# Attention turns of a retention and bilinear feed-forward kernel, rewritten as one burst of 64x64 matmuls over four quadrants of the array

## The chip, the core and the metric

The kernel runs on one core of a Trainium2 chip. A core has a matrix engine (TensorE, in the profile PE, with its weight loads as PEld), a vector engine (VectorE, DVE), a scalar engine (ScalarE, ACT), a general engine (GpSimd, POOL), a queue engine that issues transfers (SyncE, SP) and 16 DMA engines. Matmuls write into PSUM, which has eight banks of 128 partitions by 512 float32 numbers; the other engines read the banks and write into SBUF.

The metric is the time of one execution on the device in microseconds. Three executions of the kernel before gave 220.25, 220.42 and 220.65 us, a median of 220.42.

## The reference

```python
q, k, v: (4, 8, 768, 64)                       # batch, heads, sequence, head width
gamma = 1.0 - 2.0 ** (-5.0 - arange(8))
for t in range(768):                           # per batch and head
    state = gamma * state + outer(k[t], v[t])
    y[t] = (1 / 8) * q[t] @ state
x = y.transpose(0, 2, 1, 3).reshape(3072, 512)
out = ((x @ w_a) * (x @ w_b)) @ w_out          # (512, 1536), (512, 1536), (1536, 512)
```

The first half is a linear attention with a decay for each head, the second a feed-forward block without an activation function. All inputs and the output are float32; the kernel multiplies in bfloat16.

## The kernel before, in words

The sequence is cut into 24 slots of 128 tokens (4 batches of 6 slots). Instead of stepping through the tokens, the kernel folds the decay into two tables that scale keys and queries, and then works on a slot in four steps, all on PE, all with 64-wide heads:

- `scores`: keys times queries, 128 keys by 128 queries for each of 8 heads, as 16 products of 64 keys by 128 queries. They go to two PSUM banks, one for each parity `r` of the head. Then DVE multiplies each bank with a triangular mask into `aT`, so a product of a late key with an early query is computed and set to zero.
- `update`: keys times values, added to the running state `st` in PSUM (8 products, full 128 rows by 64 columns, 64 moving columns), after which an engine casts the state to `gst`.
- `inter`: the state of the slots before times the queries (8 products of 64x64, 128 moving columns), into the banks `y0` and `y1`.
- `intra`: values times the masked scores (8 products, 128 rows by 64 columns, 128 moving columns), into the same banks. `leave` then copies `y0` and `y1` with two ACT instructions to `xt`, the input of the feed-forward block.

Slots are taken in pairs. `turn(new, old)` does the scores and updates of the pair that begins with slot `new`, and the inter and intra products of the pair `old`, whose scores stem from an earlier turn. Eleven calls of `turn` carry slots 6 to 23 (pairs 3 to 11): T1 `turn(6, None)`, T2 `turn(None, 6)`, T3 `turn(8, None)`, T4 `turn(10, 8)`, T5 `turn(12, 10)`, T6 `turn(14, 12)`, T7 `turn(16, 14)`, T8 `turn(18, 16)`, T9 `turn(20, 18)`, T10 `turn(22, 20)` and T11 `turn(None, 22)`. Slots 0 to 5 go through functions of their own (`scores2`, `update2`, `inter2`, `intra2`), which this change touches in the name and the shape of one tile only.

Around the turns runs the feed-forward block over seven tiles of 4, 2, 2, 2, 2, 4 and 8 slots. `ffn_ab` is one step of it: four products into a bank for `a`, which ACT casts to `asb`, and four into a bank for `g`, which DVE multiplies with `asb` into `ht`. The tiles of two slots have 256 moving columns, those of four have 512. The output product of the middle tiles is done in seven products instead of eight (`Group`, with sums `hs` made on POOL or DVE); `single` laces one such group with the first steps of the next tile. Its arguments are the banks that it uses.

Three things set the order of the work. All instructions of an engine run in the order in which the program writes them (`seq`), so the order by hand at the end of the kernel is the order on each engine. PSUM is the second: three banks, `ff0` to `ff2`, form a ring (`Ring`) for the feed-forward products. `tile` takes the bank that has been idle longest in program order; `back` puts a bank at the end of the row as soon as the instruction that empties it has been written. The other five banks are `at0`, `at1`, `y0`, `y1` and `st`. A matmul into a bank waits on the chip until whoever emptied it is done. The third is that PE takes its matmuls in order, so a matmul that waits holds up all that follow.

Of the kernel before, what the change touches and what calls it, by code (L numbers as in the profile page):

```python
# [9 lines left out]
F32 = mybir.dt.float32  # L10
BF16 = mybir.dt.bfloat16
# [13 lines left out]
def kernel(  # L25
# [44 lines left out]
    class Ring:  # L70
# [143 lines left out]
    mask = const.tile([P, 1, P], BF16, name="mask")  # L214
    gst = [const.tile([P, HP, D], BF16, name=f"gst{i}") for i in range(4)]

    def late_tables():
        seq(nc.gpsimd.memset(mask, 1.0))
        seq(nc.gpsimd.affine_select(out=mask, in_=mask, compare_op=ALU.is_ge, fill=0.0, base=0,
                                    pattern=[[0, 1], [1, 2], [2, 64]], channel_multiplier=-1))  # L220
        tables([[P, NCH], [0, 1]], 1)
# [107 lines left out]
    def scores(t, where):  # L329
        at = score_banks(where)  # L330
        for hp in range(HP):
            for c in range(2):
                for r in range(2):
                    seq(nc.tensor.matmul(at[r][half(c), hp, :],  # L334
                                         kqT[t // 2][half(r), t % 2, 0, hp, half(c)],
                                         kqT[t // 2][half(r), :, 1, hp, half(t % 2)],
                                         start=True, stop=True, skip_group_check=True))
        aT[t] = tra.tile([P, 2, HP, P], BF16, tag="aT", name="aT")
        for r in range(2):
            seq(nc.vector.tensor_tensor(aT[t][:, r], at[r], mask.to_broadcast([P, HP, P]), op=ALU.mult))  # L340
        psff.back(*at)

    def update(t, eng):
        ci = t % NCH
        if ci == NCH - 1:
            return
        if ci == 0:
            state[0] = psst.tile([P, HP, D], F32, tag="st", name="st")
        st = state[0]
        for hp in range(HP):  # L350
            for r in range(2):
                seq(nc.tensor.matmul(st[half(r), hp, :], kb[t][:, hp, r, :],  # L352
                                     vb[t][:, HP * r + hp, :],
                                     start=(ci == 0 and hp == 0), stop=(hp == HP - 1),
                                     skip_group_check=True))
        cast(eng, gst[(t + 1) % 4], st)

    ys, begun = {}, set()

    def begin(t, *q):  # L360
        fresh = (t // 2, *q) not in begun
        begun.add((t // 2, *q))
        return fresh

    def inter(t):
        if t % NCH == 0:
            return
        for j in range(2):
            for c in range(2):
                for r in range(2):  # L370
                    hp = 2 * j + c
                    seq(nc.tensor.matmul(ys[t // 2][r][half(c), j, :, t % 2, :],
                                         gst[t % 4][half(r), hp, :],
                                         kqT[t // 2][half(r), :, 1, hp, half(t % 2)],
                                         start=begin(t, c, r), stop=False, skip_group_check=True))

    def intra(t):
        for r in range(2):
            for j in range(2):
                for c in range(2):  # L380
                    hp = 2 * j + c
                    seq(nc.tensor.matmul(ys[t // 2][r][half(c), j, :, t % 2, :],  # L382
                                         vb[t][:, HP * r + hp, :], aT[t][:, r, hp, :],
                                         start=begin(t, c, r), stop=True, skip_group_check=True))

    def leave(t):
# [5 lines left out]
        for r in range(2):  # L392
            seq(nc.scalar.copy(xt[key][:, 2 * r : 2 * r + 2, i * P : (i + 2) * P],  # L393
                               ys[t // 2][r].rearrange("p j a s n -> p j (a s n)")))

    def turn(new, old, eng=nc.scalar):
        if old is not None:
            ys[old // 2] = [psat.tile([P, 2, 2, 2, P // 2], F32, tag=f"y{r}", name="y") for r in range(2)]
        two = new is not None and (new + 1) % NCH < NCH - 1
        if new is not None:  # L400
            if two or old is None:
                update(new, eng)
            scores(new + 1, "y" if old is None else "ff")
            scores(new, "at")
        if old is not None:
            inter(old)
            inter(old + 1)
        if two:
            update(new + 1, nc.scalar)
        elif new is not None and old is not None:  # L410
            update(new, eng)
        if old is not None:
            intra(old)
            intra(old + 1)
            leave(old)


    kqT2 = {}
# [23 lines left out]
    def scores2(u, par, where="at"):  # L442
# [9 lines left out]
        aT[t] = tra.tile([P, 2, HP, P], BF16, tag="aT", name="aT")  # L452
        for r in range(2):
            seq(nc.vector.tensor_tensor(aT[t][:, r], at[r], masks[par].to_broadcast([P, HP, P]),
                                        op=ALU.mult))
# [29 lines left out]
    def intra2(u, par, begin):  # L485
# [3 lines left out]
        for hp in range(HP):  # L489
            for r in range(2):  # L490
                for c in range(2):
                    seq(nc.tensor.matmul(ys[u][c][half(r), hp, :], vb[t][half(c), 2 * hp + r, :],
                                         aT[t][half(c), r, hp, :],
                                         start=(begin and hp == 0), stop=not begin,
                                         skip_group_check=True))
# [25 lines left out]
    def ffn_a(J, ft, c0=0, c1=None):  # L521
# [11 lines left out]
        psff.back(bank)  # L533

# [89 lines left out]
    class Group:  # L624
# [141 lines left out]
    class Unit:  # L766
# [21 lines left out]
        def snap(self, n):  # L788
            pool, tag = ((tra, "aT"), (osbp, "osb"), (osbp, "osb"))[n]
            self.snaps[n] = pool.tile([P, 4 * P], F32, tag=tag, name=f"snap{n}")  # L790
# [64 lines left out]
    def big():  # L855
# [5 lines left out]
        def do(x):  # L861
            if x in plains:
                plain(*plains[x])
            elif x == "T":
                turn(None, 22)
# [131 lines left out]
    turn(6, None, V_)  # L997
# [5 lines left out]
    turn(None, 6)  # L1003
# [6 lines left out]
    turn(8, None)  # L1010
# [4 lines left out]
    turn(10, 8)  # L1015
# [35 lines left out]
    turn(16, 14)  # L1051
    blocks(4, 11, NFT)
    hsums(4, 3, 6, G_)
    casts(19)
    single(4, Y0, AT0, FF)
# [50 lines left out]
```

## Time and profile before

| what | value |
|---|---|
| time, median of three executions | 220.42 us |
| the profiled execution's own time | 220.34 us |
| its span on the core | 218.6 us |
| PE busy | 211.6 us (97%), 2242 matmuls |
| DVE, ACT, POOL busy | 138.9, 99.5 and 142.1 us |
| granted TensorE clock | full in all 40 slices |

The span runs from the first to the last instruction that the profile records; 1.7 us of the execution lie around it. In lists by line, the columns are the line of the kernel, engine, operation, tiles, shape and count, then the busy time and the mean duration of one in ns, then the idle time of the engine just before them. In a timeline each row is one run of like instructions: its start and its length in us, the engine, the line, and the count. A matmul's duration holds the time that it needs to pass through the array; the next one may start long before it ends, so the pace is read from starts, not from durations.

### The profile page before, as it was taken

How to read it: one execution, taken by the hardware profiler on the slowest of the kernel's cores; microseconds unless marked ns; L12 is line 12 of the kernel's file. 1: busy time of each engine (PE TensorE's matmuls, PEld its weight loads, DVE VectorE, ACT ScalarE, POOL GpSimd, SP SyncE). 2: the span in 40 equal slices, each digit the busy share in tenths (PEclk: the TensorE clock that was granted, in tenths of full speed). 3: DMA queues.
4: the chain of work that ended last, by engine and by line, in shares of the span. 5: the costliest groups of instructions: out<-in, count | busy, mean ns of one | idle time of the engine just before them, and what ended most of it. 6: DMA issues, size and time to landing. Idle time of an engine off the chain costs nothing.

```text
span 218.6 us, 5641 instructions
## 1 busy us (share of the span) xinstructions
PE 211.6 (97%) x2242; PEld 143.6 (66%) x2242; DVE 138.9 (64%) x253; ACT 99.5 (46%) x218; POOL 142.1 (65%) x163
## 2 busy tenths in 40 slices
PE   7789999999999999999999999999999999999994
PEld 3557445687458888888888655556865444448883
DVE  3776346845883485455377246976595777789642
ACT  3256335343234445464576245455535665632331
POOL 5265876779445587669765949999999985520000
PEclk9999999999999999999999999999999999999999
DMA  6999999999999999999999999940022000000055
GB/s 163 290 321 364 385 320 357 380 250 242 201 258 249 278 188 216 132 225 244 209 186 232 208 212 218 266 73 4 3 96 96 0 1 3 0 0 1 27 192 168
DMA packets 85146, 39.68 MB, mean 182 GB/s; under 512 B 57472, under 2 KB 78848, under 8 KB 85120
## 3 DMA queue, kind: packets, MB, share of 16 engines
q1 hardware_dynamic: 84976, 39.26, 79.9%
q8 instruction: 17, 0.28, 0.5%
q10 hardware_dynamic: 144, 0.07, 0.1%
q14 instruction: 9, 0.07, 0.1%
HBM read 28.31 MB, written 6.29 MB: 158 GB/s over the span
## 4 chain that ended last, share of the span: by engine, by line
PE 90%; SPq 4%; DMA 4%; POOL 0%; issue 0%; DVE 0%; ACT 0%
PE g L541 19%; PE a L529 19%; PE mA L645 12%; PE uA L785 8%; PE mB L645 6%; PE o L566 5%; PE uB L785 4%; DMA wstb<-in_moe_w_b_dram 4%; SPq L127 3%; PE mC L645 3%; PE at L334 2%; PE uC L785 2%; PE y L382 2%; PE st L352 2%; PE ka L844 2%; PE kb L844 2%
## 5 line engine op out<-in xcount | busy, mean ns | idle before, releaser
L543 DVE TENSOR_TENSOR ht<-g,asb 128x256 bf16<-128x256 f32 (+1 forms) x74 | 37.2, 503 | 37.1 <-PE g L541 34.2
L529 PE MATMUL a<-xt,wa_bf 128*128 128x256 bf16 (+1 forms) x296 | 52.7, 305 | 0.1
L541 PE MATMUL g<-xt,wb_bf 128*128 128x256 bf16 (+1 forms) x296 | 52.5, 304 | 0.2 <-POOL wb_bf L240 0.2
L532 ACT CAST asb<-a 128x256 bf16<-128x256 f32 (+1 forms) x74 | 32.3, 437 | 39.1 <-PE a L529 35.7
L541 PEld LDWEIGHTS <-wb_bf 128*128 128x128 bf16 x296 | 28.6, 98 | 12.8 <-POOL wb_bf L240 0.3
L529 PEld LDWEIGHTS <-wa_bf 128*128 128x128 bf16 x296 | 28.0, 98 | 12.2 <-POOL wa_bf L240 0.4
L281 POOL TENSOR_TENSOR kqb<-kf,ktab 128x512 bf16<-128x512 f32 x22 | 23.2, 1056 | 16.3 <-DMA kf<-in_k_dram 9.7
L645 PEld LDWEIGHTS <-hs 128*128 128x128 bf16 x240 | 23.4, 98 | 3.9
L340 DVE TENSOR_TENSOR aT<-at,mask 128x512 bf16<-128x512 f32 x36 | 22.3, 682 | 0.3
L791 ACT COPY snap<-uA 128x512 f32<-128x512 f32 x30 | 16.7, 587 | 12.6 <-PE uA L785 12.6
L281 POOL TENSOR_TENSOR kqb<-qf,qtab 128x512 bf16<-128x512 f32 x18 | 19.5, 1082 | 3.3 <-DMA qf<-in_q_dram 3.3
L652 ACT COPY snaps<-mA 128x256 f32<-128x256 f32 x30 | 11.2, 374 | 19.4 <-PE mA L645 19.3
L579 POOL TENSOR_TENSOR hs<-ht,hs 128x384 bf16<-128x384 bf16 (+1 forms) x17 | 16.7, 987 | 4.8 <-DVE ht L543 4.8
L645 PEld LDWEIGHTS <-ht 128*128 128x128 bf16 x180 | 17.5, 98 | 2.8
L579 POOL TENSOR_TENSOR ht<-gsb,asb 128x512 bf16<-128x512 bf16 x12 | 13.6, 1156 | 5.7 <-DVE gsb L579 5.7
L579 POOL TENSOR_TENSOR hs<-ht 128x384 bf16<-128x384 bf16 (+2 forms) x12 | 13.8, 1150 | 4.0 <-DVE ht L543 4.0
L645 PE MATMUL mA<-wsum,hs 128*128 128x256 bf16 x120 | 15.7, 273 | 0.0
L240 POOL CAST vb<-vf 128x512 bf16<-128x512 f32 x16 | 10.0, 642 | 7.4 <-DMA vf<-in_v_dram 7.2
L579 DVE TENSOR_TENSOR osb<-mB,snaps 128x256 f32<-128x256 f32 x20 | 8.4, 422 | 9.5 <-PE mB L645 5.1
L566 PE MATMUL o<-wo_bf,ht 128*128 128x512 bf16 x48 | 10.7, 379 | 0.0
L393 ACT CAST xt<-y 128x512 bf16<-128x512 f32 x18 | 9.7, 588 | 0.6 <-PE y L382 0.4
L579 DVE TENSOR_TENSOR gsb<-uB,snap 128x512 bf16<-128x512 f32 x10 | 6.9, 686 | 4.0 <-ACT snap L791 3.4
(104 smaller groups left out, 327.1 us busy)
## 6 DMA issues: line engine op xcount, KB each, us to landing
qf<-in_q_dram SPq DMA_DIRECT2D x12, 512.0 KB, 6.0
out_dram<-osb SPq DMA_DIRECT2D x21, 256.0 KB, 4.0
kf<-in_k_dram SPq DMA_DIRECT2D x18, 256.0 KB, 4.5
vf<-in_v_dram SPq DMA_DIRECT2D x18, 256.0 KB, 5.2
wsta<-in_moe_w_a_dram SPq DMA_DIRECT2D x6, 512.0 KB, 7.9
wstb<-in_moe_w_b_dram SPq DMA_DIRECT2D x6, 512.0 KB, 8.2
wsto<-in_moe_w_out_dram SPq DMA_DIRECT2D x6, 512.0 KB, 8.8
kf<-in_k_dram SPq DMA_DIRECT2D x3, 512.0 KB, 7.1
```

The lines of the kernel that those rows point to most:

```text
L281: seq(eng.tensor_tensor(dst, src, tab, op=ALU.mult))
L340: seq(nc.vector.tensor_tensor(aT[t][:, r], at[r], mask.to_broadcast([P, HP, P]), op=ALU.mult))
L529: seq(nc.tensor.matmul(a, wa_bf[:, kt, fs], xcols(J, kt, c0, c1), start=(kt == 0), stop=(kt == KT - 1)))
L532: seq(nc.scalar.copy(asb, a))
L541: seq(nc.tensor.matmul(g, wb_bf[:, kt, fs], xcols(J, kt, c0, c1), start=(kt == 0), stop=(kt == KT - 1)))
L543: seq(nc.vector.tensor_tensor(ht[J][:, ft, c0:c1], g, asbs.pop((J, ft, c0)), op=ALU.mult))
L566: seq(nc.tensor.matmul(o, ht[J][:, ft, i * P : (i + 1) * P], wo_bf[:, ft], start=(ft == 0), stop=(ft == NFT - 1), skip_group_check=True))
L579: seq(eng.tensor_tensor(dst, x, y, op=op))
L645: seq(nc.tensor.matmul(m, w, right[:, j], start=(first and j == 0), stop=(j == NP - 1), skip_group_check=True))
L652: seq(nc.scalar.copy(self.snaps[:, n], self.bank["A"]))
L785: seq(nc.tensor.matmul(m, w, right[:, k], start=(first and k == 0), stop=(k == 1), skip_group_check=True))
L791: seq(nc.scalar.copy(self.snaps[n], self.bank["A"]))
```

## The change

A turn becomes one `Burst`. Each of its products is 64 rows by 64 columns, so that four fit in the array at once: two halves of rows (keys, or heads for products that contract over the head width) by two halves of columns. The program keeps a list for each of the four quadrants (a lane), and `issue` writes the products in the order in which four clocks, one for each lane, reach them (56 for a product of 128 moving columns, 32 for one of 64).

- The scores: a product has 64 queries instead of 128. For each head and slot there are two products on the diagonal (`at`) and one of early keys with late queries (`off`, in two more banks); late keys with early queries are left out. That makes 48 products of 64 columns for a pair in place of 32 of 128. ACT copies each `off` bank to `aT`; DVE multiplies each `at` bank, which now holds both slots, with a mask `tri` of 64 columns: two DVE instructions for a pair in place of four.
- The intra products contract over 64 keys instead of 128: 40 products for a pair (8 of 128 columns and 32 of 64) in place of 16 of 128 columns with 128 rows. Part of the early values is copied to the other half of the partitions by two DVE copies for a pair (`early`).
- The first update of a turn joins the burst as 16 products of 64 rows; a second one follows the burst as before, and the cast of the state after it is put off to the next `ffn_a` or `turn` (`later`, `catch_up`).
- Products of the two row halves must not write a bank at the same time. A `token` is a product of 4 columns into a bank taken from the ring; from the second token on, the bank is taken anew (`renew`), so that the token waits for the one before. Between two row halves in a bank lie at least two tokens.
- Where a turn has both a new and an old pair (T4 to T10), the two `off` banks come from the ring, as does the bank of the tokens, which is taken first. In T1 and T3 `off` uses `y0` and `y1`.
- `leave` copies `y0` with ACT and `y1` with DVE, but with ACT alone in T2 and T11. Slots 7 and 9 are updated one turn later. T7 moves behind the last step and the sums of its tile, directly before `single(4, ...)`, whose banks `AT0` and `Y0` change places.
- In the last group of the kernel the two halves of the last row go to two tiles `osb` in place of one; two tiles take other buffers (`aT2`, `snap`).

```diff
+        def renew(self, old, shape, dtype, name):
+            n = next(n for n, (x, _) in enumerate(self.out) if x is old)
+            tag = self.out[n][1]
+            self.out[n] = ffpool.tile(shape, dtype, tag=tag, name=name), tag
+            return self.out[n][0]
...
-    mask = const.tile([P, 1, P], BF16, name="mask")
+    tri = const.tile([P, 1, 64], BF16, name="tri")
...
+    class Burst:
+        def __init__(self):
+            self.lists = {(row, c): [] for row in range(2) for c in range(2)}
+            self.left, self.then = {}, {}
+            self.spot = psff.tile([P, 4], F32, tag="ff", name="token")
...
+        def token(self, row, c):
+            def make():
+                if self.tokens:
+                    self.spot = psff.renew(self.spot, [P, 4], F32, "token")
+                return nc.tensor.matmul(self.spot[half(c)], ident[half(row), half(c)], ident[half(row), :4],
+                                        start=True, stop=True, skip_group_check=True)
...
+        def issue(self):
+            clock = {x: 0 for x in self.lists}
+            self.tokens, user = 0, {}
+            while any(self.lists.values()):
+                lane = min((x for x in self.lists if self.lists[x]), key=lambda x: (clock[x], x))
+                bank, cols, make, what = self.lists[lane].pop(0)
+                clock[lane] += 56 if cols > 64 else 32
+                if bank is None:
+                    continue
+                seq(make())
...
+                row, since = user.get(bank, (lane[0], 0))
+                assert row == lane[0] or self.tokens >= since + 2, (bank, what)
...
+            psff.back(self.spot)
...
+        def scores(self, u, row, at, off, hps=range(4)):
...
+            for hp in hps:
+                for s in range(2):
+                    for c in range(2):
+                        self.add(row, c, f"at{row}", 64,
+                                 product(at[row][half(c), hp, s], s, hp, c, c), ("S", row))
+                    self.add(row, hp // 2, f"off{row}", 64,
+                             product(off[row][half(hp // 2), hp % 2, s], s, hp, 0, 1), ("S", row))
...
+        later.append(lambda: cast(nc.scalar, gst[(t + 1) % 4], state[0]))
...
-        for r in range(2):
-            seq(nc.scalar.copy(xt[key][:, 2 * r : 2 * r + 2, i * P : (i + 2) * P],
-                               ys[t // 2][r].rearrange("p j a s n -> p j (a s n)")))
-
-    def turn(new, old, eng=nc.scalar):
+        for r, eng in enumerate(on):
+            cast(eng, xt[key][:, 2 * r : 2 * r + 2, i * P : (i + 2) * P],
+                 ys[t // 2][r].rearrange("p j a s n -> p j (a s n)"))
+
+    def turn(new, old, updates=None, eng=nc.scalar, on=(nc.scalar, nc.vector)):
+        catch_up()
+        x = Burst()
...
+        if new is not None:
+            u = new // 2
+            offs = score_banks("ff" if old is not None else "y")
...
+            def left(r):
+                seq(nc.scalar.copy(aT[u][:, r, HP:], off[r]))
+                seq(nc.vector.tensor_tensor(aT[u][:, r, :HP].rearrange("p h s n -> p (h s) n"),
+                                            at[r].rearrange("p h s n -> p (h s) n"),
+                                            tri.to_broadcast([P, 2 * HP, 64]), op=ALU.mult))
+                if old is not None:
+                    psff.back(offs[r])
...
+        for row in range(2):
+            if new is None:
+                x.inter(old, row)
+                x.inter(old + 1, row)
+                x.intra(o, row, row)
+                x.token(row, row)
+                x.rest(row, 1 - row)
+                x.intra(o, row, 1 - row)
+                continue
+            if row == 0:
+                if first is not None:
+                    x.update(first, 0, "u0")
+                    x.token(0, 0)
+                if old is not None:
+                    x.intra(o, 0, 1)
+                    x.token(0, 1)
+                x.scores(u, 0, at, off)
+            else:
+                if old is not None:
+                    x.intra(o, 1, 0)
+                x.scores(u, 1, at, off, range(1))
+                if old is None:
+                    x.scores(u, 1, at, off, range(1, HP))
+                if first is not None:
+                    x.token(1, 1)
+                    if old is None:
+                        x.rest(1, 0)
+                    x.update(first, 1, "u0")
+                if old is not None:
+                    x.scores(u, 1, at, off, range(1, HP))
+                    x.token(1, 0)
+            if old is not None:
+                x.inter(old, row)
+                x.inter(old + 1, row)
+                x.intra(o, row, row)
+        x.issue()
+        if second is not None:
+            update(second)
+        if new is not None:
+            for s in range(2):
+                src = vb[new + s][:64].rearrange("p (r hp) d -> p r hp d", r=2)[:, :, 2:]
+                seq(nc.vector.tensor_copy(early[u][64:, s], src))
+        if old is not None:
+            leave(old, on)
...
-                    c = slice(DH + n * P, DH + (n + 1) * P)
-                    cast(eng, self.row(0)[:, c], self.bank["A"][:, n * P : (n + 1) * P])
-                    seq(queue.dma_start(out=last_row[:, c], in_=self.osb[0][:, c]))
+                    c = slice(n * P, (n + 1) * P)
+                    osb = osbp.tile([P, P], F32, tag="osb", name="osb")
+                    cast(eng, osb, self.bank["A"][:, c])
+                    seq(queue.dma_start(out=last_row[:, DH + n * P : DH + (n + 1) * P], in_=osb))
...
-    turn(16, 14)
     blocks(4, 11, NFT)
     hsums(4, 3, 6, G_)
+    turn(16, 14)
     casts(19)
-    single(4, Y0, AT0, FF)
+    single(4, AT0, Y0, FF)
```

More of the change, by code (lines that the diff above doesn't have):

```diff
@@ L350, in update @@
+    def update(t):
         for hp in range(HP):
             for r in range(2):
[L352 to L354 removed]
+                seq(nc.tensor.matmul(state[0][half(r), hp, :], kb[t][:, hp, r, :],
+                                     vb[t][:, HP * r + hp, :], start=False, stop=(hp == HP - 1),
                                      skip_group_check=True))
[L356 removed]
@@ L358 @@
[L358 to L375, printed above, removed]
@@ L387, in leave @@
+    def leave(t, on):
         J, i = where[t]
@@ L400, in turn @@
+        x.issue()
+        if second is not None:
+            update(second)
         if new is not None:
[L401 to L404, printed above, removed]
+            for s in range(2):
+                src = vb[new + s][:64].rearrange("p (r hp) d -> p r hp d", r=2)[:, :, 2:]
+                seq(nc.vector.tensor_copy(early[u][64:, s], src))
         if old is not None:
-            inter(old)
@@ L407, in turn @@
[L407 to L418, printed above, removed]
+            leave(old, on)
+    kqT2, aT2 = {}, {}
     def casts2(u, on, between=None):
```

142 lines of the change are left out of this document (100 added, 42 removed).

## The prediction

> **What bounds the kernel now.** I read the page first (span, busy shares, granted clock), then the busy time by stretch, then the timeline of PE over single turns. The first fence is from the page, the second from the table of stretches.
>
> ```profile
> span 218.6 us, 5641 instructions
> ...
> PE 211.6 (97%) x2242; PEld 143.6 (66%) x2242; DVE 138.9 (64%) x253; ACT 99.5 (46%) x218; POOL 142.1 (65%) x163
> ...
> PEclk9999999999999999999999999999999999999999
> ```
>
> ```profile
> 66.00:121.00 55.00, 55.00 (x773) 47.88 (x772) 31.07 (x65) 28.36 (x72) 38.29 (x40) 1.00 1.25 216
> 121.00:149.00 28.00, 28.00 (x334) 15.30 (x333) 17.53 (x28) 12.74 (x25) 24.37 (x29) 1.00 1.01 185
> ```
>
> In a row of stretches the third number is PE's busy time: PE is never without a matmul in the stretches that hold T3 to T10, and its clock is full. So every lane step and every wait on PE moves the end by its own length. All other engines have a third of their time free and matter only by when they free a bank.
>
> The timeline of PE in T5 gives the paces; the last two rows, from the same view, are an update of the opening in 64x64 products and T8's start.
>
> ```profile
> 96.22 0.60 PE L541 MATMUL g<-xt,wb_bf 128*128 128x256 bf16 x4
> 96.75 0.32 PE L352 MATMUL st<-vb,kqb 128*64 128x64 bf16 x8
> 96.99 0.64 PE L334 MATMUL at<-kqT 64*64 64x128 bf16 x32
> 97.47 0.39 PE L372 MATMUL y<-kqT,gst 64*64 64x128 bf16 x16
> 97.79 0.32 PE L352 MATMUL st<-vb,kqb 128*64 128x64 bf16 x8
> 97.94 0.62 PE L382 MATMUL y<-aT,vb 128*64 128x128 bf16 x16
> 98.48 0.39 PE L529 MATMUL a<-xt,wa_bf 128*128 128x256 bf16 x2
> ...
> 15.84 0.42 PE L469 MATMUL st<-vb,kqb 64*64 64x64 bf16 x16
> ...
> 133.28 0.81 PE L541 MATMUL g<-xt,wb_bf 128*128 128x512 bf16 x3
> 134.03 0.32 PE L352 MATMUL st<-vb,kqb 128*64 128x64 bf16 x8
> ```
>
> ```profile
> L334 PE MATMUL at<-kqT 64*64 64x128 bf16 x288 | 6.0, 219 | 0.0
> L382 PE MATMUL y<-aT,vb 128*64 128x128 bf16 x144 | 5.6, 220 | 0.0
> L352 PE MATMUL st<-vb,kqb 128*64 128x64 bf16 x120 | 4.7, 201 | 0.0
> L372 PE MATMUL y<-kqT,gst 64*64 64x128 bf16 x120 | 3.3, 218 | 0.0
> L469 PE MATMUL st<-vb,kqb 64*64 64x64 bf16 x48 | 1.3, 193 | 0.0
> ```
>
> *Pace.* A row's length less one duration, over its steps less one, is the pace of a lane. L382 runs two lanes, eight steps: (0.62 - 0.22) / 7 = 0.057 us. L469, two lanes, eight steps of 64 columns: (0.42 - 0.193) / 7 = 0.032. I take 0.056 and 0.032. L334 has four lanes and eight steps in the 0.48 us to the next row, so four quadrants really run at once (32 x 0.056 would be 1.79).
>
> *Switch of shape.* The g row has starts (0.60 - 0.27) / 3 = 0.109 apart; a fifth would come at 96.66, the turn comes at 96.75: 0.09 lost. The first step after a switch is about 0.025 longer (0.48 against 8 x 0.056 = 0.45). I take 0.12 for a switch.
>
> **The sum before.** From the counts above, steps per lane: scores 288 / 4 x 0.056 = 4.03, inter 120 / 4 x 0.056 = 1.68, intra 144 / 2 x 0.056 = 4.03, updates 120 / 2 x 0.032 = 1.92, together 11.7. The eleven turns have 39 switches (four in T5: to 128x64, to 64x64, back, out): 4.7. Sum 16.3 us. Check on T5: 1.38 of steps and 0.48 of switches make 1.86; the rows give 98.48 - 96.66 = 1.82.
>
> **The sum after, lanes alone.** In a full burst the lanes of row 1 are longest: 4 update steps, 12 of scores and 12 of intra (28 x 0.032 = 0.90), 4 of inter (0.22), a token (0.03): 1.15 us. T4, T5, T7, T8, T10: 5.76. T6 and T9 lack an inter slot (the first slot of a batch): 2 x 1.04. T1 and T3: 16 steps and a token, 2 x 0.54. T2 0.53, T11 0.64. Together 10.1. Six second updates (4 x 0.032 each): 0.8. Switches: two for each of eleven bursts and one more for each second update, 28 x 0.12 = 3.4. Sum 14.2, so **2.1 us less**. The products that are left out and the row-split of intra pay for this; the switches give 1.3 of it.
>
> **The wait for the second off bank.** This is the step that turns the sign. At a turn's start the ring has the bank of the last-but-one g first, then the last a's, then the last g's. Before, the scores took the first two. Now the token bank takes the first, `off[0]` the second, and `off[1]` the bank of the g product that has just left PE. DVE must empty that first. The fence shows DVE's part of the timeline at T5, then at T8, then the chain of waits where PE starts on a release by POOL.
>
> ```profile
> 96.93 0.42 DVE L543 TENSOR_TENSOR ht<-g,asb 128x256 bf16<-128x256 f32 x1 [0.45 <-PE g L541]
> 97.46 2.48 DVE L340 TENSOR_TENSOR aT<-at,mask 128x512 bf16<-128x512 f32 x4
> ...
> 134.20 0.69 DVE L543 TENSOR_TENSOR ht<-g,asb 128x512 bf16<-128x512 f32 x1 [1.03 <-PE g L541]
> ```
>
> ```profile
> 18.55 0.62 POOL wb_bf L240
> 19.22 0.61 PE g L541 x4
> ```
>
> A release reaches PE 0.05 us after its end (19.17 to 19.22). So the bank is free at 97.35 + 0.05 = 97.40 in T5, 0.65 after the burst's start at 96.75; in T8 at 134.94, 0.91 after 134.03. The first product into `off[1]` stands in lane (1, 0) behind 6 intra steps and one score: 7 x 0.032 + 0.025 = 0.25 into the burst. PE takes matmuls in order, so all four lanes stop: 0.40 us in T4 to T7, 0.66 in T8 to T10. Together **3.6 us**. Bounds: nothing, if the bank's user were already done; 0.65 and 0.91 if the product came first.
>
> **The tokens.** From the second on, each waits for the one before. No row shows PE waiting for itself at such a distance. A matmul of 64 columns lasts 193 ns, of 128 columns 219, which makes about 169 at 4 columns, and 0.05 for the signal: 0.22 us. The lower bound is the pace lost at a switch, 0.12, which is the array running empty; the upper one 0.26, the same with a whole 128-column duration. In a full burst the tokens stand at lane times 0.13, 0.26, 0.30 and 0.70. The second lies behind the bank wait, so it finds the first one long done. The third comes 0.05 after the second: 0.22 - 0.05 = 0.17, say 0.19 with the last product's rest. The fourth waits for nothing. T2 and T11 have one such wait of 0.2 each; T1 and T3 have one token and no wait. 7 x 0.19 + 0.4 = **1.7 us**.
>
> **Behind the burst.** DVE has less to do: two masks (0.68 each) in place of four, but one copy of y (about the 0.69 of a 512-column DVE row) and two small ones. ACT loses a y copy and gains two of 256 columns. What feeds on them: in T7, `single(4)` now starts at once and in `AT0`, which DVE has to mask first. The scores of row 0 end at lane time 0.72, with lead and waits 1.33; plus 0.19 of matmul, 0.11 until DVE starts (96.82 to 96.93), 0.68 and 0.05 gives 2.36, against a burst that is out, switch included, at 1.88: **0.45 us**. In T6 the third step behind the burst takes the bank of a g that stands in DVE's queue behind masks and copies: 0.2 more. Small gaps of before near T5 and T10 go: 0.1 less. Together about 0.55. The second update waits for ACT's cast of the state, but the bank wait covers that.
>
> The mask's set-up on POOL and `aT2` lie before 18.55, where PE waits for weights: nothing. Updates of slots 7 and 9 only change turns: same steps. The `snap` tile has three buffers instead of four and lives six of seven steps: nothing. DMA issues are the same.
>
> The tail: the split of `osb` may let DVE copy beside ACT.
>
> ```profile
> 215.41 0.27 ACT L238 COPY osb<-mA 128x128 f32<-128x128 f32 x1 [1.59 <-PE mA L645]
> 215.70 0.29 DVE L240 COPY osb<-mA 128x128 f32<-128x128 f32 x1 [0.53 <-ACT osb L238]
> ```
>
> DVE starts when ACT is done. Both write one tile, but both also read one bank, and the new code still reads one bank. I take nothing, with 0.29 as the bound. The Trainium skill (PSUM — Partial Sum Buffer, section PSUM bank collisions raise a hardware error) says that two engines must not even read the same bank and partitions at once, so the two would stay in a row. The trace agrees with that order but can't tell which of the two reasons set it.
>
> **Sum.** -2.1 + 3.6 + 1.7 + 0.55 = +3.75, on the profiled execution's 220.34: 224.1 us. The profiled execution lies 0.08 under the median of 220.42, which I leave out.
>
> **The rivals.**
> *Faster: the waits inside a burst cost next to nothing.* Place: PE's queue at the first product into `off[1]` and at the third token. For it: DVE is a third idle, and PE never waited in a turn so far. Against: the 0.65 and 0.91 are read off rows. Without any wait the sum is -2.1 + 0.55: 218.8. It decides once a full burst waits less than 1.55 / 7 = 0.22 us in all.
> *The bank is free, the tokens are not.* Then the second token waits too, 0.09: 7 x 0.28 + 0.4 = 2.4, -2.1 + 2.4 + 0.5 = +0.8: 221.1.
> *PE's queue can't feed four lanes of 64 columns.* The trace's fastest long stretch is L334, 32 matmuls and as many weight loads in 0.48 us, 7.5 ns each; a full burst wants 248 in 1.15, 4.6 ns each. At 7.5 ns it takes 1.86, 0.71 more, so 7 x 0.71 and about 1.3 in the other four: at most +6.3, of which the waits hide up to 4.1. That gives 226.3 to 230. Against: L334's lanes were full, so 7.5 is their pace and no limit seen. The Trainium skill (TensorE: Matmul & The Clock Gate, section Wait — 56ns, not 53.3ns?) puts the least distance of two matmul starts at about 25 ns; the trace disagrees for the array as a whole, with 15 ns in L334.
> *It cancels:* gains and waits within 0.2%.
>
> **How the numbers follow.** 0.2% (0.44 us) is about what a measurement of this kernel can tell from no change. Forecast 0.57, faster 0.18, bank free 0.12, queue 0.08, cancelled 0.05. Slower holds the forecast, the bank case and the queue case: 0.77. The forecast's own range is 222.4 to 225.4 (tokens at 0.12 to 0.26, the bank wait and the lanes off by 0.35 each). For 8 in 10 the range goes down into the faster case and up to the queue case: 219.2 to 226.2.
>
> **What would show it.** In T4 to T10 the gap in PE's matmuls about 0.25 us into the burst, of 0.40 and 0.66 us, ending right behind a DVE row of L543; a second one of 0.17 at the third token; the stretches no longer full; scores, intra and updates in steps of 0.032 between them; PE waiting for DVE's mask behind T7. It is wrong if the bursts run through without a hole, or if the steps are longer than 0.032 with none.

## The result, and the profile after

The changed kernel takes **227.17 us** (median of four runs, 227.05 to 227.34) against 220.39 for the kernel before on the same chip: a ratio of 1.0307, with a 95% interval of 1.0289 to 1.0325. It is slower, as forecast, but by 6.8 us where 3.75 were forecast, and it lies outside both ranges.

The page of the profile of the kernel after:

```profile
span 225.4 us, 6584 instructions
...
PE 212.8 (94%) x2699; PEld 144.5 (64%) x2710; DVE 141.2 (63%) x260; ACT 100.8 (45%) x229; POOL 141.4 (63%) x164
...
PEclk9999999999999999999999999999999999999999
```

The table of stretches (the third number is PE's busy time):

```profile
66.00:121.00 55.00, 52.95 (x940) 45.67 (x940) 29.11 (x64) 27.21 (x74) 37.77 (x39) 1.00 1.11 214
121.00:149.00 28.00, 25.60 (x440) 15.11 (x432) 16.90 (x27) 12.45 (x28) 21.15 (x26) 1.00 1.05 190
```

The clock is full as before. PE's busy time is nearly what it was (212.8 against 211.6), and the span is 6.8 us longer. PE now stands idle for 2.05 us of the first stretch and 2.40 of the second, in which it never stood before. What came in is waiting.

The timeline of PE over one burst, T5 (rows are left out at the dots). The last three rows stand behind later bursts: T6, T7 and T8.

```profile
97.21 0.22 PE L403 MATMUL st<-vb,kqb 64*64 64x64 bf16 x2
...
97.42 0.20 PE L411 MATMUL at<-kqT 64*64 64x64 bf16 x2
97.44 0.22 PE L439 MATMUL y<-aT,vb 64*64 64x128 bf16 x1
97.86 0.22 PE L411 MATMUL at<-kqT 64*64 64x64 bf16 x2 [0.20 <-DVE ht L682]
...
97.92 0.17 PE L368 MATMUL token<-ident 64*64 64x4 bf16 x1
...
97.95 0.19 PE L403 MATMUL st<-vb,kqb 64*64 64x64 bf16 x1
98.19 0.16 PE L368 MATMUL token<-ident 64*64 64x4 bf16 x1
...
98.31 0.48 PE L411 MATMUL at<-kqT 64*64 64x64 bf16 x35
98.59 0.18 PE L368 MATMUL token<-ident 64*64 64x4 bf16 x1
...
99.40 0.28 PE L667 MATMUL a<-xt,wa_bf 128*128 128x256 bf16 x1
...
116.12 0.60 PE L667 MATMUL a<-xt,wa_bf 128*128 128x256 bf16 x4 [0.63 <-DVE ht L682]
...
122.09 0.82 PE L784 MATMUL mA<-wo_bf,ht 128*128 128x256 bf16 x6 [0.37 <-DVE aT L498]
...
144.16 1.02 PE L667 MATMUL a<-xt,wa_bf 128*128 128x512 bf16 x4 [0.50 <-DVE ht L682]
```

Read from the top. A quarter of a microsecond into the burst PE stops, and goes on at 97.86 when DVE has read the bank of the last g (`<-DVE ht`; DVE's row ends at 97.80): the wait for `off[1]`. At 97.95 it stops again; the third token starts 0.27 behind the second. Then 35 score products start within 0.28 us, 8 ns apart, in four lanes: 0.032 us for a step of a lane. The last three rows are waits **behind** bursts: T6 and T8 for a bank that DVE has still to read, T7 for DVE's mask.

DVE's timeline behind T5 shows why it is late:

```profile
98.85 1.29 DVE L498 TENSOR_TENSOR aT<-at,tri 128x512 bf16<-128x512 f32 x2 [1.04 <-PE at L411]
100.17 1.59 DVE L550 COPY early<-vb 64x256 bf16<-64x256 bf16 x2
101.79 0.69 DVE L248 CAST xt<-y 128x512 bf16<-128x512 f32 x1
102.40 0.75 DVE L682 TENSOR_TENSOR ht<-g,asb 128x256 bf16<-128x256 f32 x2
```

Before, DVE's four masks in T5 began 0.71 us after the turn did (97.46 against 96.75) and ended 1.46 after PE had left it. Now there are two, but they begin 1.64 after the burst did (98.85 against 97.21), because the scores are spread over all lanes to near the burst's end; with copies and the cast of y behind them DVE comes to the next product with g 3.00 after PE has left the turn (102.40 against 99.40).

To sort the 6.8 us I took, for each of the eleven turns, the time from the last matmul start in front of it to the first behind it. In T5 that is 98.485 - 96.547 = 1.94 before and 99.401 - 97.004 = 2.40 after. The sums are 18.14 and 22.56, so 4.4 us came in within the turns and 2.4 between them. A "gap" here is the distance of two matmul starts less the usual step.

| step of the prediction | forecast | measured | from |
|---|---|---|---|
| wait for `off[1]` | +3.6 | +3.3 | gaps 0.349, 0.360, 0.362, 0.361 in T4 to T7, 0.629, 0.628, 0.629 in T8 to T10 |
| tokens | +1.7 | +1.9 | 0.205 at the third token of seven bursts, 0.22 in T2, 0.25 in T11 |
| lanes and switches | -2.1 | -1.45 | 4.42 less the two above, less T7's 0.44 (its gap of 0.53 less 0.09 for the switch) and T11's 0.22 |
| behind the burst | +0.55 | +3.0 | T7's 0.44, T11's 0.22 and the 2.4 between the turns |

The gaps between the turns: 0.36 behind T4, 0.40 behind T5, 0.80 behind T6, 0.45 behind T7 (a second one), 0.67 behind T8, less about 0.3 for small gaps of before that are gone. T11's 0.22 stands in front of its first product into `y1`, at 159.92: DVE's cast of that bank, behind T10's two copies of 2.28 us, ends at 159.86.

### The profile page after: what moved, and what is told of

Its sections match the earlier page's. It is cut to its first block, busy times and chain, and to the rows that moved or that the text cites. A ratio compares the mean times of both kernels' runs of the same rounds, so it can differ in the third digit from the quotient of the medians.

```text
span 225.4 us, 6584 instructions
## 1 busy us (share of the span) xinstructions
PE 212.8 (94%) x2699; PEld 144.5 (64%) x2710; DVE 141.2 (63%) x260; ACT 100.8 (45%) x229; POOL 141.4 (63%) x164
## 4 chain that ended last, share of the span: by engine, by line
PE 46%; DVE 5%; issue 1%; ACT 1%; DVEq 0%; ACTq 0%
PE mA L784 9%; PE uA L925 7%; PE a L667 6%; PE g L680 6%; PE mB L784 4%; PE uB L925 3%; PE mC L784 2%; DVE ht L682 2%; PE uC L925 2%; PE kb L985 2%; PE ka L985 2%; PE at L411 1%; DVE early L550 1%; DVE aT L498 1%; DVE xt L248 1%
## 5 line engine op out<-in xcount | busy, mean ns | idle before, releaser
L289 POOL TENSOR_TENSOR kqb<-qf,qtab 128x512 bf16<-128x512 f32 x18 | 18.8, 1042 | 4.1 <-DMA qf<-in_q_dram 4.1
L498 DVE TENSOR_TENSOR aT<-at,tri 128x512 bf16<-128x512 f32 x18 | 11.6, 686 | 9.7 <-PE at L411 9.6
L411 PE MATMUL at<-kqT 64*64 64x64 bf16 x432 | 8.8, 195 | 2.2 <-DVE ht L682 2.0
L246 ACT CAST xt<-y 128x512 bf16<-128x512 f32 x15 | 8.6, 597 | 3.5 <-PE y L630 2.2
```

Source lines behind the costliest of these rows:

```text
L289: seq(eng.tensor_tensor(dst, src, tab, op=ALU.mult))
L498: seq(nc.vector.tensor_tensor(aT[u][:, r, :HP].rearrange("p h s n -> p (h s) n"), at[r].rearrange("p h s n -> p (h s) n"), tri.to_broadcas ...
```

## The experiments

Each starts from the kernel after. The g-kernels pile up: g1 holds the edit of e1, g2 that of g1, and so on up to g5; g6 is said below. Lines of an edit that are left out are marked by dots. The numbers in brackets are the 95% intervals of the ratio to the kernel before.

**e1: the early copies on ACT.** The copies of `vb` into `early` go from DVE to ACT, one behind each asb copy, for T4 to T10.

```
-                seq(nc.vector.tensor_copy(early[u][64:, s], src))
+                if old is None:
+                    seq(nc.vector.tensor_copy(early[u][64:, s], src))
+                else:
+                    later.append(lambda s=s, src=src: seq(nc.scalar.copy(early[u][64:, s], src)))
...
+        if new == 22:
+            catch_up()
```

> The changed kernel with the two copies into the early tile taken off DVE: in the turns T4 to T10 ACT makes them, put off behind the casts of the next steps (for T10 right behind the turn). Theory: DVE's queue behind a burst (masks 1.29, the two copies 0.43 to 1.6, the y1 copy 0.69) is what PE waits for behind T4 to T8, 2.7 us in all (gaps of 0.36, 0.40, 0.80, 0.45 and 0.67). Without the copies the y1 copy ends 0.4 to 1.6 us earlier, so the waits behind T4, T5, T7 (for xt) and T8 go and the one behind T6 shrinks by about 0.5: 227.2 - 2.4 = 224.8 us. Rival (DVE's queue isn't what PE waits for, or the y1 copy alone is enough to hold it up): the gaps stay, 226.7 or more.

Measured: 225.37 us, 1.0227 [1.0212, 1.0242]. The gaps behind T4, T5 and T8 and T7's second are gone, T6's fell to some 0.3: about 2.4 us in all. But a wait of 0.76 came behind T3, whose two copies were left on DVE. DVE's and POOL's timelines of this kernel there:

```profile
78.11 1.59 DVE L551 COPY early<-vb 64x256 bf16<-64x256 bf16 x2
79.73 1.09 DVE L687 TENSOR_TENSOR ht<-g,asb 128x256 bf16<-128x256 f32 x3
```

```profile
77.58 1.04 POOL L289 TENSOR_TENSOR kqb<-kf,ktab 128x512 bf16<-128x512 f32 x1
78.58 1.04 POOL L289 TENSOR_TENSOR kqb<-qf,qtab 128x512 bf16<-128x512 f32 x1
```

The same two copies took 0.73 us in the kernel after. Here they end at 79.70, when POOL's second row (to 79.62) is over. The first a behind T3 had to wait for DVE's rows behind them. So the copies are no "small ones", and their length has to do with POOL.

**e2: the wait for `off[1]` taken away.** In the last step in front of each of T4 to T10 the product with g is left out: ACT copies asb to `ht`, so that no engine reads the bank of the last g.

```
+        if (J, ft) in ((2, 10), (3, 9), (4, 5), (4, 11), (5, 5), (5, 8), (5, 11)):
+            seq(nc.scalar.copy(ht[J][:, ft, c0:c1], asbs.pop((J, ft, c0))))
+        else:
             seq(nc.vector.tensor_tensor(ht[J][:, ft, c0:c1], g, asbs.pop((J, ft, c0)), op=ALU.mult))
```

> The changed kernel in which the last feed-forward step before each of T4 to T10 leaves out the product with g: its g matmuls run as before, but nobody reads the bank; ACT writes the cast a to ht in place of DVE's multiplication. So the bank of off[1] is free as soon as PE has left it. Theory: the seven gaps at the first product into off[1] (0.35 to 0.63 us, 3.3 in all, and some 0.05 each of restarting lanes) go, and in return the second token now waits for the first, about 0.09 each: 227.2 - 3.3 - 0.35 + 0.65 = 224.2 us. Rival (the gap there is something else, such as PE's queue running dry in the burst): the gap stays or moves a few products on, 226.5 or more.

Measured: 224.76 us, 1.0201 [1.0184, 1.0219]. The timeline of PE at the same place in T5, and behind T8:

```profile
97.48 0.20 PE L411 MATMUL at<-kqT 64*64 64x64 bf16 x2
...
97.54 0.19 PE L411 MATMUL at<-kqT 64*64 64x64 bf16 x1
97.69 0.16 PE L368 MATMUL token<-ident 64*64 64x4 bf16 x1
...
97.91 0.16 PE L368 MATMUL token<-ident 64*64 64x4 bf16 x1
...
143.16 1.02 PE L667 MATMUL a<-xt,wa_bf 128*128 128x512 bf16 x4 [0.54 <-DVE ht L685]
```

PE runs through the first score, and the gap of 0.36 is gone: it was the bank. The second token, which lay in the bank's shadow, now waits 0.12 itself (one of the rivals had 0.09), and the third 0.13 in place of 0.205. Bursts that end sooner meet the same late DVE: the gaps behind T6, T7 (the second) and T8 are now 1.07, 0.79 and 0.71, where they were 0.80, 0.45 and 0.67. In T4 a gap of 0.49 stays, for the transposed `kqT`. Of 3.3 us only 2.4 came back.

**e3: the third token later.** Two groups of scores go in front of it.

```
                     x.intra(o, 0, 1)
+                    x.scores(u, 0, at, off, range(2))
                     x.token(0, 1)
-                x.scores(u, 0, at, off)
+                    x.scores(u, 0, at, off, range(2, HP))
...
```

> The changed kernel with the third token of a full burst moved four to eight score products back in its lane, so that it comes some 0.18 us of lane time behind the second token in place of 0.05. Theory: a token waits until 0.24 us after the one before it (97.92 to 98.18 in T5 of the changed kernel); the gap of 0.205 at the third token falls to about 0.07 in each of T4 to T10: 227.2 - 7 x 0.14 = 226.2 us. Rival (the gap isn't the wait for the second token but for something that stays in its place, such as the state's bank): unchanged, 227.2.

Measured: 227.79 us, 1.0340 [1.0318, 1.0362]: no gain on the kernel after (1.0307), and rather a loss. The token's gap fell from 0.205 to 0.08 in all seven bursts, which are 0.9 us shorter together, as expected: it was a wait for the token before. (Tokens that wait stand 0.27 apart here too, not 0.24 as the text above has it.) But the gap behind T8 grew from 0.67 to 1.38 (its two copies took 2.06 us and not 1.52), and one of 0.76 came behind T3, with copies of 1.59 us as in e1. A shift of tenths on PE decides how a copy meets POOL.

**e4: T7 at its old place**, in front of the last g steps of group 4, with the banks of `single(4)` in their old order.

```
+    turn(16, 14)
     blocks(4, 11, NFT)
     hsums(4, 3, 6, G_)
-    turn(16, 14)
     casts(19)
-    single(4, AT0, Y0, FF)
+    single(4, Y0, AT0, FF)
```

> The changed kernel with T7 at the place where it was before (ahead of the tile's last step) and the banks of the group behind it as before (Y0, AT0). Theory: of the time lost around T7, 0.44 us is PE waiting for DVE's mask in AT0 and 0.45 waiting for DVE's copy into xt; at the old place a step and a group's products lie between, so both go, and some 0.2 comes back as a wait for a bank of the ring: 227.2 - 0.7 = 226.5 us. Rival (the place of T7 makes no difference, the waits only change their names): 227.0 to 227.4.

Measured: 227.39 us, 1.0314 [1.0298, 1.0330], level with the kernel after, as the rival had it. T7's two gaps (0.53 and 0.45) went, one of 0.24 came for a bank that ACT has to empty. What was gained there went elsewhere: T4's scores waited 0.96 for the transposed `kqT`, which POOL's cast had fed late because a load of q had come late. That wait lies 40 us in front of T7; this run can't say whether the edit caused it. The price of T7's place is read from g4 below.

**g1: T3's early copies on ACT too** (only T1's stay on DVE). **g2: g1, and the second and third tokens spaced out** (three score groups in front of the one, two in front of the other).

```
-                if old is None:
+                if new == 6:
                     seq(nc.vector.tensor_copy(early[u][64:, s], src))
...
                     x.intra(o, 0, 1)
+                    x.scores(u, 0, at, off, range(3))
                     x.token(0, 1)
-                x.scores(u, 0, at, off)
+                    x.scores(u, 0, at, off, range(3, HP))
...
-                x.scores(u, 1, at, off, range(1))
+                x.scores(u, 1, at, off, range(2))
...
```

> As e1 (the copies into the early tile made by ACT behind T4 to T10), and now behind T3 too, where one of DVE's copies held up a product for 0.76 us in e1. Theory: these copies on DVE stand still while POOL works, so how long they take is a matter of where POOL is, and in e1 the copy behind T3 happened to fall badly: 225.4 - 0.75 = 224.6 us. Rival (the gap behind T3 stems from something else that ends late there, such as the masks): 225.4.

> g1 with the second and the third token of a full burst moved back among the scores (lane times 0.13, 0.32, 0.50, 0.74 in place of 0.13, 0.26, 0.30, 0.70). Theory: in e3 the wait at the third token went, and what it gave was eaten by DVE's queue behind the burst, which the early copies made long; with these on ACT the gain reaches the end: 7 x (0.20 + 0.05 for lanes that start anew) = 1.7 less than g1, so 222.9 us. Rival (the later state and the later scores only push the same time behind the burst): within 0.3 of g1.

Measured: g1 225.22 us, 1.0218 [1.0200, 1.0236]; g2 224.96, 1.0202 [1.0186, 1.0219]. Both missed. In g1 the wait behind T3 is not gone but made anew. ACT's timeline:

```profile
77.78 0.40 ACT L675 CAST asb<-a 128x256 bf16<-128x256 f32 x1
78.21 0.40 ACT L553 COPY early<-vb 64x256 bf16<-64x256 bf16 x1
78.64 0.37 ACT L675 CAST asb<-a 128x256 bf16<-128x256 f32 x1
79.03 0.40 ACT L553 COPY early<-vb 64x256 bf16<-64x256 bf16 x1
79.46 0.37 ACT L675 CAST asb<-a 128x256 bf16<-128x256 f32 x1
```

`three(2, 7)` issues three a's in a row, and each asb now stands behind a copy: PE waits 0.32 and 0.39. On ACT each of these copies takes 0.40. In g2 the gaps of 0.205 went, and the fourth token, now close behind the third, waits 0.17 in each burst.

**g3: diagonal scores first, off products last** in each row's list, so that both off banks are wanted only when DVE has long read them, and the tokens lie further apart. **g4: g3 with T7 at its old place**, as in e4.

```
-                    x.scores(u, 0, at, off, range(3, HP))
+                    x.scores(u, 0, at, off, range(3, HP), "a")
+                    x.scores(u, 0, at, off, range(HP), "o")
...
-                    x.scores(u, 1, at, off, range(2, HP))
+                    x.scores(u, 1, at, off, range(2, HP), "a")
+                    x.scores(u, 1, at, off, range(HP), "o")
...
```

> g2 in which a full burst makes the diagonal scores first and the products into the two off banks last, so that the first product into off[1] comes at 0.6 us of lane time in place of 0.25. Theory: the bank is free 0.65 us into the burst with steps of 256 columns and 0.91 with 512, so the gap goes in T4 to T7 (0.40 each) and shrinks to about 0.25 in T8 to T10 (by 0.4 each): 2.8 less than g2, 220.1 us. But the second token, which the gap had covered, may now wait 0.05 each: 220.5. Rival (the gap moves along with the products): within 0.5 of g2.

> g3 with T7 back at its old place and the banks of the group behind it as before. Theory: PE no longer waits 0.5 us for DVE's mask in AT0; some 0.2 comes back as a wait for ACT's copy of the first off bank, since no second update follows in T7: 0.3 less than g3. That makes 219.9 to 220.2 us, level with the kernel before or just under it. Rival: no change against g3 (within 0.1).

Measured: g3 221.42 us, 1.0062 [1.0026, 1.0098]; g4 221.59, 1.0060 [1.0038, 1.0082]. The order of the lists, on top of g2, is worth 3.5 us, more than the 2.8 expected: no gap within a full burst is over 0.15 any more. T7's gap is down to 0.37 in g3, from 0.41 in g2 and 0.53 in the kernel after; moved back, it gives that for a 0.24 behind ACT, and the times are level: g4's expected gain of 0.3 did not come.

**e6: the early copies as reductions.** On the kernel after alone: the same elements, engine and places, but a maximum over an axis of one element in place of a copy.

```
-                seq(nc.vector.tensor_copy(early[u][64:, s], src))
+                seq(nc.vector.tensor_reduce(out=early[u][64:, s].rearrange("p r c (d o) -> p r c d o", o=1),
+                                            in_=src.rearrange("p r c (d o) -> p r c d o", o=1),
+                                            op=ALU.max, axis=mybir.AxisListType.X))
```

> The edit, on the kernel after alone: the eighteen early copies stay on DVE at their places, and are made with a reduction over an axis of one element (maximum) in place of a copy, so the same 64x256 elements go through. A (the copies stand still while POOL holds something that a copy needs, and a reduction does not need it): every one of the eighteen takes the same, about 0.3 us (an estimate: 256 of the 512 elements that take 0.69 us in L682, 0.35), with POOL at work or not, where the copies took 0.21 to 1.19. The gaps behind the bursts then change with what DVE's queue gains or loses there: T5 0.40, T7's second 0.45 and T8 0.67 go, T4 grows by 0.28 and T6 by about 0.13, so 1.1 us less: 226.1 us (225.7 to 226.5). B (the copies are long for their shape or because SBUF is busy, whoever works): the reductions spread in the same way, up to 1 us and more, and the time stays at 227.1 to 227.3.

Measured: 226.02 us, 1.0260 [1.0247, 1.0274], where A had 226.1. The durations (least, median, most, in ns) of the copies in the kernel after, and of the reductions in this one, from the view of one line's instructions:

```profile
L550 DVE COPY early<-vb x18: 211/464/1190, 63.0 to 158.0; 64x256 bf16<-64x256 bf16 x18
```

```profile
L550 DVE TENSOR_REDUCE early<-vb x18: 402/408/413, 63.0 to 156.5; 64x256 bf16<-64x256 bf16 x18
```

A reduction needs twice as long as a copy at its best, but at most 0.413 us. All the spread is gone, with POOL as busy as in the kernel after (141.8 us against 141.4). The gap behind T5 and T7's second went, T8's fell from 0.67 to 0.28; T4's and T6's grew, as forecast, to 0.74 and 0.97. So the copies were long because they were copies beside a busy POOL, not because of their shape or place, and that is worth 1.1 us here.

**g5: g4, with the bank of the tokens given out first behind a burst, and T3's copies behind the third asb. g6: the same ring, with T1's and T3's copies made as reductions on DVE.**

```
             psff.back(self.spot)
+            psff.idle.insert(0, psff.idle.pop())
...
+        held_back.append(1)
         for f in range(ft, ft + 3):
             ffn_a(J, f)
+        held_back.clear()
         for f in range(ft, ft + 3):
             ffn_g(J, f)
+        catch_up(2)
```

(`held_back` keeps `ffn_a` from issuing the copies.) In g6, in place of the second part:

```
-                if new == 6:
-                    seq(nc.vector.tensor_copy(early[u][64:, s], src))
+                if new in (6, 8):
+                    seq(nc.vector.tensor_reduce(...))
```

> The edit, on g4 (early copies by ACT, tokens spaced, off products last, T7 at its old place): behind T3 ACT's two early copies come after the third asb and not between them, and the bank of the tokens is the next that is given out behind a burst, in place of the first off bank, which ACT has still to empty. A (what g4 has left above the kernel before are the waits of 0.32 and 0.39 behind T3 for asb, of 0.24 behind T7 and 0.13 in front of T6's first a): all four go, 221.59 less 1.08 gives 220.5 us, level with the kernel before (220.39) within 0.4. B (DVE's or ACT's queue gives part back at the next place, as it did when single waits were taken away from the kernel after): 221.0 to 221.6.

> As g5, but the early copies of T1 and T3 are made by DVE as reductions (those of the other turns by ACT), and nothing is held back in front of asb. A: reductions of about 0.35 us each end behind T3's mask before the first g there is done, so the waits of 0.32 and 0.39 go as in g5: 220.5 us within 0.4, level with g5. B: the two reductions, 0.7 us in DVE's queue behind the mask, hold the first product with g there, and its wait of some 0.3 us takes the place of the others: 0.3 over g5.

Measured: g5 220.56 us, 1.0019 [1.0007, 1.0031]; g6 220.61, 1.0028 [1.0010, 1.0045]. Both come out as A had it. The table of stretches of g5, and DVE's timeline behind its T5:

```profile
66.00:121.00 55.00, 54.91 (x1009) 48.56 (x1008) 27.73 (x59) 32.93 (x89) 38.28 (x40) 1.00 1.18 216
121.00:149.00 28.00, 27.79 (x450) 15.49 (x452) 16.40 (x25) 14.79 (x33) 24.05 (x28) 1.00 0.98 184
```

```profile
97.82 1.29 DVE L501 TENSOR_TENSOR aT<-at,tri 128x512 bf16<-128x512 f32 x2 [0.40 <-PE at L412]
99.03 0.68 DVE L248 CAST xt<-y 128x512 bf16<-128x512 f32 x1
99.70 0.42 DVE L696 TENSOR_TENSOR ht<-g,asb 128x256 bf16<-128x256 f32 x1
```

PE is full again in both stretches but for 0.3 us. The masks begin 1.00 us into the burst (97.82 against 96.82, the start of T5) and the next product with g starts 1.15 after PE has left it (99.70 against 98.55); in the kernel after these were 1.64 and 3.00. The small costs that made the 6.8 us are undone to 0.2 or 0.3%. The kernel before isn't beaten, though: with the visible waits gone the eleven turns sum to 18.27 us, against 18.14 before.

## Why the prediction was wrong in size

**What bounds the kernel; the pace.** Right. PE is the bound, its clock full, and a lane step of 64 columns takes 0.032 us in four quadrants too. The measured time lies in the span of the rival in which PE's queue can't feed four lanes (226.3 to 230), but its mechanism is refuted: its 1.86 us for the 124 products of a burst are 15 ns for each, and the 35 scores start 8 ns apart.

**The wait for the second off bank.** Right in place, cause and nearly in size (0.36 for 0.40, 0.63 for 0.66); e2 takes it away, and it goes. In T4 the transposed `kqT` lands at the same moment, so that there either would do. The rival by which the waits cost next to nothing falls with it.

**The tokens.** Right at the third (0.205 for 0.19) and in T2 and T11. Tokens that wait stand 0.27 apart (97.92 to 98.19), at the upper end that the prediction gave. That the second one would wait too, were the bank free, is what e2 shows with 0.12.

**Behind the burst.** This is the step that failed: +0.55 forecast, +3.0 measured, four fifths of the miss. Its first term, T7's mask, was right (0.45, though the figures given for it make 0.48; measured 0.44). What was wrong is the sentence that DVE has less to do, "one copy of y ... and two small ones". Two things were missed. First, it counted DVE's work and not when that work starts: the masks begin 1.64 us into the turn and not 0.71, so less work ends later. Secondly, the small copies took 0.21 us only where POOL was at rest or between two rows. In T10 DVE's and POOL's timelines of the kernel after read:

```profile
156.86 2.28 DVE L550 COPY early<-vb 64x256 bf16<-64x256 bf16 x2
```

```profile
156.80 1.14 POOL L718 TENSOR_TENSOR hs<-ht 128x512 bf16<-128x512 bf16 x1
157.91 1.15 POOL L718 TENSOR_TENSOR hs<-ht,hs 128x512 bf16<-128x512 bf16 x1
```

Each of the two copies lasts as long as one row of POOL. Of the 18 copies in the kernel after eight took 0.21 or 0.22 us; the other ten took 0.44 to 1.19, and each of these ended 0.08 to 0.09 us behind the end of a row of POOL. So did all 32 longer ones in e1 to e4.

The Trainium skill (SBUF — State Buffer, section Who interferes with whom) says that a copy or cast on DVE in a two-port mode shares a port pair with GpSimd (POOL in the profile), that whichever issues first holds it for its whole instruction, that the other is blocked and not slowed, and that a reduction on this chip has no such mode. The traces agree on each point that they can show: copies of 0.21 us and copies that end with a row of POOL, reductions of 0.40 to 0.41 beside a busy POOL. That it is this port pair, no run here shows. Taken off DVE altogether (e1), the copies free about 2.4 us of gaps; made insensitive to POOL (e6), 1.1.

The two causes fall on different turns. In DVE's timeline of the kernel after the copies behind T4 and T6 read:

```profile
83.32 0.36 DVE L550 COPY early<-vb 64x256 bf16<-64x256 bf16 x2
...
114.44 0.57 DVE L550 COPY early<-vb 64x256 bf16<-64x256 bf16 x2
```

They are at rest or nearly so, and yet PE waits 0.36 and 0.80 there: DVE's queue as a whole, which starts late, is too long. In T5, T7 and T8 the copies take 1.59, 1.49 and 1.52, over 1.1 more than in T4, which is more than the gaps (0.40, 0.45 and 0.67). In e6 these three went or shrank, and those behind T4 and T6 did not. No run moved the masks' start and nothing else.

The prediction named T6 and T7 and left out T4, T5, T8 and T11, which DVE's queue reached as well.

**The lanes alone.** -2.1 forecast, -1.45 measured: most of the rest of the miss. The sum before was good (16.3; the eleven turns' 18.14 less the eleven steps in front of them, 1.73, make 16.4). The one after takes the longest lane as the burst's time. But PE takes its products in one order, and a lane that waits or restarts holds the others: T9 in g5, without the bank wait, still takes 1.47 us from its first start to that of the second update behind it (141.06 to 142.53), where its longest lane has 1.04 and the switch 0.12. In it stand distances of 0.13, 0.12 and 0.06 us between starts, where all others are at most 0.05. How these divide between tokens and lanes of unequal length is open; no run separated them, since without tokens two lanes would write one bank unguarded.

**The tail.** Rightly put at nothing. DVE's copy still starts when ACT's is done, though they write two tiles now (ACT's and DVE's timeline of the kernel after):

```profile
222.15 0.27 ACT L246 COPY osb<-mA 128x128 f32<-128x128 f32 x1 [1.64 <-PE mA L784]
...
222.45 0.29 DVE L248 COPY osb<-mA 128x128 f32<-128x128 f32 x1 [0.57 <-ACT osb L246]
```

So of the two reasons that the prediction left side by side, the common tile is out, and the common bank is left.

## What to carry to other kernels

When work for the bound engine is woven more tightly, look at when its last result leaves, not only at its length: the engine behind it starts later, and everything in its queue moves, though it has less to do. A copy on DVE like the ones here has no price of its own while POOL works; look at its least and most in the trace, and where it stands in front of something urgent, try it on ACT or as a reduction. And the waits inside the bursts went best by reordering what was there (3.5 us in g3, with the copies off DVE already), while taking away one wait at a time (e2, e3, g1, g2) mostly uncovered the next.

## What was not expected of the hardware

A 64x256 bf16 copy on DVE took 0.21 us or up to 1.19, and each long one ended just behind a row of POOL; the same as a reduction took 0.40 to 0.41 each time, and on ACT 0.40. Hence small shifts on PE changed single gaps by 0.7 us at places that the edit didn't touch: whether POOL left a hole of 0.06 us between two rows (78.55 to 78.61 in the kernel after) decided whether T3's copies took 0.73 or 1.59 (e1 and e3, without a hole). Four lanes of 64x64 tiles started a product every 8 ns, with no sign of a limit of PE's queue.
